# Lead pair of an attention and affine-MLP kernel: another order of two weight sums, one block cast by its own load, batch 3 loaded and flipped at other places, and its a2 blocks turned by TensorE

## The chip, the core and the metric

The kernel runs on one NeuronCore of a Trainium2 chip. A core has five engines with instruction streams of their own: TensorE (PE, with its weight loads as PEld), VectorE (DVE), ScalarE (ACT), GpSimd (POOL) and SyncE (SP, which here only issues transfers). Transfers run on 16 DMA engines; those issued by SP go to the hardware queue q1, those issued by POOL to the software queue q0, which also cast float32 to bfloat16 on the way and can add to what is in DRAM. The metric is the time of one launch in microseconds, the median of several runs.

## What is computed

Grouped attention for 8 batches (16 query heads, 4 key and value heads, 384 tokens, head size 64), and behind it one layer of a residual MLP with affine norms:

```python
scores = scale * np.matmul(q, k.transpose(0, 1, 3, 2))
attn = softmax(scores);  x = attn @ v                    # (8, 384, 1024)
a1 = alpha1 * x + beta1
tok = np.einsum('ts,bsd->btd', w_tok, a1)
u = x + lam * tok
a2 = alpha2 * u + beta2
ch = np.maximum(a2 @ w_ch1, 0.0) @ w_ch2                 # 1024 -> 4096 -> 1024
out = u + lam * ch
```

(`softmax` stands for the four lines that subtract the maximum, exponentiate, sum and divide.) The two channel products are most of the arithmetic.

## The kernel before

**Pairs.** Batches are taken two at a time. For a pair, each of the two channel products is done with seven half-size products in place of eight, the scheme of Strassen and Winograd: the two batches are the two row blocks of the left matrix, and the weight matrix has four blocks, for W2 named "11", "12", "21", "22" (half of the 4096 rows, half of the 1024 columns). The right-hand sums are S5 = B12 - B11, S6 = B22 - S5, S7 = S6 - B11 and S4 = B21 - S6. `sum_w2(o, c)` (L491) makes quarter c of S_o on DVE with one subtraction (L494), in place: S5 and S6 overwrite B12, S7 overwrites B11, S4 overwrites a second copy of B21, named "again". Then `keep_w2` (L488, issued at L489 on SP) stores the quarter to a DRAM buffer w2s, from which pairs 2 to 4 load all seven right-hand matrices. The plain blocks B11 and B22 are stored too. So the lead pair makes the sums, and the later pairs only fetch them.

**The lead pair.** Attention of batches 0 and 1 runs ahead, up to about 68 us. The first product of the pair (`first_product`, matmuls at L635) follows, then the second product (`second_product`, matmuls at L706, C<-...), which takes the seven products in the order S1 (B11), B21, S5, B22 as o = 3, S6, S7, S4 in 21 turns of 16 matmuls with 512 columns each. Between them the attention of the *next* pair, batches 2 and 3, is woven in: `side(b)` gives the places of the score matmuls (L254), of `av` (L289), of the token mix `tok` (L318, L322), and of what turns its result a2 over so that channels are on partitions. `pair(0)` yields after every four matmuls of the second product, and a hand-written plan, `put(ps, phase, place, function, arguments)`, says what is recorded at each yield. Here ps is the pair, phase 0 its first and phase 1 its second product. Places of batch 2's side are counted from 0, those of batch 3 from 38. The order on every engine is the order in which this plan records the instructions; nothing is reordered later. An engine waits at its own next instruction, so what is behind that instruction waits too.

**Slots.** Weights sit in six ring slots (tile w) and three pad slots, 512 KB each. `pump()` hands a freed slot to the next entry of one queue: the W1 chunks of the first product, the quarters of "21", "12", "22" and "again", then the first four W1 chunks of pair 2 (0, 8, 1, 9). B11 goes to a home of its own in the arena. A slot is freed when the last matmul that reads it is recorded, or in `last_w2` when S4's quarter has been made from it.

**B12's quarters.** `cast_w2("12", c)` (L474, on POOL, in the first product) copies a quarter from the float32 weights into a DRAM buffer raw12 as bfloat16; `load_w2` (L484, on SP) brings it from there to a slot. "21" and "again" work the same way, from w2s. "11" and "22" are cast by their own load, on POOL (L486).

**Batch 3.** Nine loads (`load_next`, L430, POOL) bring keys, queries and values. `flip_q` (L174) and `flip_k` (L170) transpose them by DMA, issued on SP. The token result u is spilled to DRAM (L221, SP), and a2 = u * alpha2 (L328) is turned over in one of two ways: by a DMA transpose on SP (L331), or by three TensorE transposes (`turn`, L392) and an ACT copy out of PSUM (L394). For batch 3 the last three of eight blocks are turned by TensorE, for batch 2 none. `sums_a` (L442 to L444, DVE) makes pair 2's left-hand sums from the turned blocks; it is put at places 76, 79 and 81. `sum_w1` (L505, L510, DVE) makes pair 2's first right-hand sums from W1 chunks.

**Results.** `scaled` multiplies a finished block by lam on POOL (L744) and adds it to the output with an accumulating transfer (L436, POOL).

Of the kernel before, what the change touches and what calls it, by code (L numbers as in the profile page):

```python
# [13 lines left out]
def kernel(  # L14
# [21 lines left out]
    nc = tc.nc  # L36
    f32 = mybir.dt.float32
    bf = mybir.dt.bfloat16
# [11 lines left out]
    P = 128  # L50
    NST = S // P
    NDT = DM // P
    NNT = DFF // P
    NDW = DM // 512
    NP = Hq // 2
    D1 = D + 1
    CW = 2
# [37 lines left out]
    turn, a2_turn = [0], [0]  # L95
# [20 lines left out]
    snaps = hTf.bitcast(f32)  # L116
    SLOTS = 7 * NH // 4
    w2s = [tc.dram_tile([P, NDT * CW * P], bf, name=f"w2s{i}") for i in range(SLOTS)]
    raw12 = [tc.dram_tile([P, NDT * CW * P], bf, name=f"raw12_{i}") for i in range(4)]
    PLACE2 = {o: i for i, o in enumerate((1, 2, 6, 5, 3, 7, 4))}  # L120

    def by_tok(ap):
# [85 lines left out]
    def side(b):  # L208
        vb = vt[b % 2]
        ess, avs, a1s, a2s, xr = {}, {}, {}, {}, {}  # L210
        first, fold = b < 2, b < 4
# [167 lines left out]
        def flip(p):  # L379
            if not first:  # L380
                spill(p)
            if not by_pe(p):
                a2_transpose(p)

        def by_pe(p):
            return b == 0 or b % 2 and p >= NP - (4 if first else 3)

        def turn(p, tag="tp"):
            ps = tp_ps([P, NST, P], tag) if first else three()[:, 0].rearrange("p a b -> p (a b)").bitcast(bf)[:, :S].rearrange(
# [9 lines left out]
        at = {}  # L399

        def put(k, *m):
            at.setdefault(k, []).append(m)
# [3 lines left out]
        for p in range(NP):  # L406
            put((4, 10, 14, 18, 24, 29, 33, 35)[p], av, p)
            put((8, 15, 17, 22, 27, 32, 36, 38 if b % 2 else 39)[p], tok_flip, p)
            if by_pe(p):
                put((36, 39, 41)[p - NP + 3], turn, p)  # L410
        return at

    def loads(b):
# [49 lines left out]
    def home(c):  # L463
        return arena[:, HOME + c * 2048:HOME + (c + 1) * 2048]

    def w2_block(name, c):
        kh, dw = int(name[0]) - 1, int(name[1]) - 1
        return w2src[:, kh * NH + 4 * c:kh * NH + 4 * c + 4, dw * 512:(dw + 1) * 512]

    def stored(name, c):  # L470
        return raw12[c] if name == "12" else w2s[4 * PLACE2[2] + c]

    def cast_w2(name, c):
        nc.gpsimd.dma_start(out=stored(name, c).rearrange("p (a c) -> p a c", a=4), in_=w2_block(name, c))  # L474

    def load_w2(name, c, slots=None):
        if slots is None:
            raw[name, c] = None, home(c)
        else:
            slot = slots.pop(0)  # L480
            raw[name, c] = slot, place(slot)
        at = raw[name, c][1]
        if name in ("21", "again", "12"):
            nc.sync.dma_start(out=at, in_=stored(name, c))  # L484
        else:
            nc.gpsimd.dma_start(out=at.rearrange("p (a c) -> p a c", a=4), in_=w2_block(name, c))  # L486

# [29 lines left out]
    def place(slot):  # L517
        return ring[:, slot] if slot < RING else pad[:, (slot - RING) * 2048:(slot - RING + 1) * 2048]
# [20 lines left out]
    order0 = EARLY + (0, 1, 2, 3, 4)  # L539
    chunks0 = [*EARLY, *(g + NCH // 2 for g in EARLY), *(c for g in order0[3:] for c in (g, g + NCH // 2))]  # L540
    queue = [(load_w1, c) for c in chunks0[RING:]] + [(load_w2, "21", c, w1_free) for c in range(4)]
    for name, cs, slots in (("12", (0, 1), w1_free), ("12", (2, 3), pad_free), ("22", (0,), pad_free), ("22", (1, 2, 3), w1_free),
                            ("again", (0,), w1_free), ("again", (1,), pad_free), ("again", (2, 3), w1_free)):
        queue += [(load_w2, name, c, slots) for c in cs]
# [356 lines left out]
    with tc.manual_schedule(engines=order):  # L901
# [122 lines left out]
        def put(ps, phase, at, *m):  # L1024
            plan.setdefault((ps, phase, at), []).append(m)

        def put_all(ps, phase, table, at=lambda u: u):
            for u, ms in table.items():
                for m in ms:
                    put(ps, phase, at(u), *m)  # L1030

        def put_flips(ps, phase, b, places):
            for u, m in zip(places, ((flip_k, b), *((flip_q, b, i, 2) for i in range(0, NP, 2)))):
                put(ps, phase, u, *m)
# [13 lines left out]
        put(1, 0, 35, to_all, 1, 1, 1)  # L1048
        put(1, 0, 38, scale_beta)
        for c in range(4):  # L1050
            put(0, 0, 1 + 3 * c, cast_w2, "12", c)
            put(0, 0, 62 + 9 * c, load_w2, "11", c)
            put(0, 1, 29 + 4 * c, keep_w2, 1, c)
            put(0, 1, 38 + 2 * c, keep_w2, 3, c)
            put(0, 1, (11, 12, 16, 18)[c], sum_w2, 5, c)
            put(0, 1, (20, 21, 25, 26)[c], sums_first_hid, 2, c)
            put(0, 1, (28, 30, 31, 34)[c], sums_first_hid, 4, c)
            put(0, 1, (37, 40, 41, 43)[c], sum_w2, 6, c)
            put(0, 1, (44, 45, 49, 50)[c], sums_first_hid, 3, c)
            put(0, 1, (51, 54, 58, 61)[c], sum_w2, 7, c)  # L1060
            put(0, 1, (57, 59, 63, 66)[c], last_w2, c)
        for u, o in ((77, 5), (79, 7), (81, 6)):
            put(0, 1, u, sum_w1, 0, o)
        for ps in range(NB - 1):
            c = 2 * ps + 2
            for i in range(9):
                put(ps, 0, 4 + 6 * i if ps == 0 else 4 + 7 * i, load_next, c, 1)
                put(ps, 1 - (ps > 0), 6 + 2 * i if ps == 0 else 91 + 2 * i, load_next, c + 1, 1)
            put_flips(ps, 0, c, range(76, 86, 2))
            put_all(ps, 1, side(c))  # L1070
            for u, f, h in zip((24, 25, 27, 29, 33, 34) if ps == 0 else (10, 17, 18, 28, 33, 33),
                               (flip_q, flip_k, flip_q, flip_q, flip_k, flip_q), (0, 0, 2, 4, 2, 6)):
                put(ps, 1, u, f, c + 1, h, 2)
            put_all(ps, 1, side(c + 1), lambda u: u + 38)
            for j, u in ((0, 76), (2, 79), (3, 81)):
                put(ps, 1, u, sums_a, j, 1 if j else 2)

        def steps(ps):
            done = [0, 0]
            for second in pair(ps):  # L1080
                for f, *a in plan.pop((ps, second, done[second]), []):
                    f(*a)
                done[second] += 1
                yield
            for key in [k for k in plan if k[0] == ps]:
                for f, *a in plan.pop(key):
                    f(*a)

        first = steps(0)

        def product(n=1):
            for _ in range(n):
                next(first)

        A, C = side(0), side(1)
        lower, upper = range(NP // 2), range(NP // 2, NP)
        A.k_transpose(0, 1)
# [20 lines left out]
        for i, c in zip((28, 30, 32, 34), range(4)):  # L1118
            at.setdefault(i, []).append((cast_w2, "21", c))
# [44 lines left out]
```

## Time and profile before

| | us |
|---|---|
| median of three runs | 763.64 |
| the runs | 757.52, 763.64, 763.93 |
| the profiled execution | 757.84 |
| its span, first to last instruction | 756.1 |
| attention of batches 0 and 1 | up to about 68 |
| lead pair, first product | 68 to 133.6 |
| lead pair, second product with attention of batches 2 and 3 | 133.6 to 251 |
| pair 2 (first and second product) | 251 to 434 |
| pair 3, pair 4 | 434 to 607, 607 to 756 |

A line of the profile names the line of the kernel, the engine, the operation and its tiles, written `out<-in`. "Idle before" is the time that an engine stood before the instruction, and the releaser is what ended it. `SPq`, `POOLq` and so on are the engine's own queue: waits and transfers being issued. The granted clock is the share of full speed that TensorE had. DMA share is the mean busy share of the 16 DMA engines; it can be over 1 because packets of two queues overlap. Tile names are shortened: `a` is a1, `k` is k2, `raw` is raw12, `w` is the ring of weight slots, `pad` the three pad slots, `obuf` holds a2 blocks, `ops` the turned left-hand operands, and `in_moe_w_ch_dram` is either of the weight matrices in DRAM.

### The profile page before, as it was taken

How to read it: one execution, taken by the hardware profiler on the slowest of the kernel's cores; microseconds unless marked ns; L12 is line 12 of the kernel's file. 1: busy time of each engine (PE TensorE's matmuls, PEld its weight loads, DVE VectorE, ACT ScalarE, POOL GpSimd, SP SyncE). 2: the span in 40 equal slices, each digit the busy share in tenths (PEclk: the TensorE clock that was granted, in tenths of full speed). 3: DMA queues.
4: the chain of work that ended last, by engine and by line, in shares of the span. 5: the costliest groups of instructions: out<-in, count | busy, mean ns of one | idle time of the engine just before them, and what ended most of it. 6: DMA issues, size and time to landing. Idle time of an engine off the chain costs nothing.

```text
span 756.1 us, 14435 instructions
## 1 busy us (share of the span) xinstructions
PE 720.0 (95%) x5644; PEld 410.1 (54%) x5703; DVE 547.3 (72%) x1016; ACT 369.6 (49%) x555; POOL 201.0 (27%) x242
## 2 busy tenths in 40 slices
PE   8997999997979799999999999999999999999998
PEld 4664555454535355655555566655555556654444
DVE  8888876485787498756968988765967888762454
ACT  7875766544525266663433266674433356660000
POOL 8753340251025254120002244120102213100011
PEclk9999999999999899999999999999999999999999
DMA  9999999999999999996999999996999999937965
GB/s 165 186 228 241 196 175 233 220 219 172 284 294 262 219 178 186 201 247 166 261 265 161 215 155 176 207 237 207 229 261 183 206 155 132 140 127 282 283 185 104
DMA packets 208465, 155.85 MB, mean 206 GB/s; under 512 B 92685, under 2 KB 186229, under 8 KB 208141
## 3 DMA queue, kind: packets, MB, share of 16 engines
q0 software_dynamic: 118064, 64.47, 65.4%
q1 hardware_dynamic: 89644, 90.01, 44.0%
q8 instruction: 44, 0.72, 0.4%
q10 hardware_dynamic: 688, 0.46, 0.2%
q14 instruction: 25, 0.20, 0.1%
HBM read 157.32 MB, written 41.94 MB: 264 GB/s over the span
## 4 chain that ended last, share of the span: by engine, by line
PE 71%; issue 9%; DVE 7%; DMA 7%; POOL 5%; ACT 1%; POOLq 0%; DVEq 0%; ACTq 0%
PE C L851 27%; PE X L785 15%; PE Y L785 8%; DMA w<-in_moe_w_ch_dram 5%; PE Z L785 4%; PE sc L254 3%; PE C L706 3%; PE sc L289 2%; PE sc L318 2%; PE X L635 2%; PE Y L635 2%; DMA pad<-w2s 1%; DMA ops<-obuf 1%; DVE pad L510 1%; POOL w L183 1%
## 5 line engine op out<-in xcount | busy, mean ns | idle before, releaser
L851 PE MATMUL C<-w,arena 128*128 128x512 bf16 (+2 forms) x711 | 163.7, 372 | 1.6 <-issue 0.3
L263 ACT ACTIVATE es<-sc 128x1024 bf16<-128x1024 f32 x108 | 104.1, 1024 | 121.5 <-PE sc L254 112.9
L851 PEld LDWEIGHTS <-arena 128*128 128x128 bf16 x1040 | 94.7, 98 | 100.6 <-issue 5.1
L436 POOL DMA_DIRECT2D out_dram<-hT x45 | 40.0, 888 | 296.7 <-DVE hT L744 138.1
L790 ACT ACTIVATE hT<-X,bias 128x384 f32<-128x384 f32 x144 | 83.6, 581 | 65.5 <-PE X L785 54.9
L785 PEld LDWEIGHTS <-w 128*128 128x128 bf16 x768 | 75.3, 98 | 56.5 <-DVE w L505 3.2
L183 POOL DMA_DIRECT2D w<-in_moe_w_ch_dram x64 | 60.0, 987 | 152.7 <-DVE xr L325 46.9
L785 PEld LDWEIGHTS <-pad 128*128 128x128 bf16 x576 | 56.8, 99 | 39.6 <-issue 3.0
L785 PE MATMUL X<-ops,pad 128*128 128x384 bf16 x384 | 71.5, 330 | 0.0
L785 PE MATMUL X<-ops,w 128*128 128x384 bf16 x384 | 70.2, 326 | 1.0 <-DVE ops L804 1.0
L851 PE MATMUL C<-pad,arena 128*128 128x512 bf16 (+2 forms) x288 | 69.5, 373 | 0.4
L706 PEld LDWEIGHTS <-arena 128*128 128x128 bf16 x336 | 30.6, 99 | 40.6 <-issue 12.9
L325 DVE TENSOR_TENSOR xr<-sc,xr 128x384 f32<-128x384 f32 x48 | 26.5, 553 | 32.4 <-PE sc L322 18.1
L318 PEld LDWEIGHTS <-wtokT 128*128 128x128 bf16 x576 | 39.0, 98 | 15.4 <-issue 3.2
L785 PE MATMUL Y<-ops,w 128*128 128x384 bf16 x192 | 40.5, 333 | 5.2 <-DVE w L505 2.8
L510 DVE TENSOR_TENSOR pad<-w,pad 128x1024 bf16<-128x1024 bf16 x64 | 44.3, 692 | 0.1
L706 PE MATMUL C<-w,arena 128*128 128x512 bf16 x161 | 41.0, 383 | 2.3 <-DMA w<-in_moe_w_ch_dram 1.8
L254 PE MATMUL sc<-qT,kT 64*128 64x384 bf16 (+2 forms) x504 | 38.0, 275 | 4.9 <-DMA kT<-k 2.4
L792 DVE TENSOR_TENSOR arena<-Y,hT 128x384 bf16<-128x384 f32 x48 | 26.5, 556 | 17.8 <-ACT hT L790 15.8
L785 PE MATMUL Z<-ops,w 128*128 128x384 bf16 x192 | 39.0, 326 | 0.0
L289 PEld LDWEIGHTS <-es 128*128 128x128 bf16 x864 | 32.8, 97 | 11.3
L263 ACT ACTIVATE hT<-sc 128x1024 bf16<-128x1024 f32 x36 | 35.7, 1036 | 4.4 <-PE sc L254 4.3
(181 smaller groups left out, 1143.1 us busy)
## 6 DMA issues: line engine op xcount, KB each, us to landing
w<-in_moe_w_ch_dram POOLq DMA_DIRECT2D x67, 512.0 KB, 10.6
w<-w2s SPq DMA_DIRECT2D x67, 512.0 KB, 4.9
pad<-w2s SPq DMA_DIRECT2D x25, 512.0 KB, 4.8
out_dram<-hT POOLq DMA_DIRECT2D x45, 256.0 KB, 7.0
out_dram<-xr SPq DMA_DIRECT2D x48, 192.0 KB, 6.1
q_raw<-in_q_dram POOLq DMA_DIRECT2D x28, 192.0 KB, 8.5
w2s<-w SPq DMA_DIRECT2D x10, 512.0 KB, 4.6
w2s<-arena SPq DMA_DIRECT2D x8, 512.0 KB, 9.5
```

Of the source, the lines that this page charges most:

```text
L183: nc.gpsimd.dma_start(out=w1[:, w1_slots[c]], in_=w1src[:, :, c * CW * P:(c + 1) * CW * P])
L254: nc.tensor.matmul(out=sc[:, hh, k % 4:k % 4 + n], lhsT=kT_[r, 2 * p // G, BLK[hh][sk], :], rhs=qT_[r, p, st:st + n, :], start=True, stop= ...
L263: nc.scalar.activation(out=e, in_=sc, func=EXP, scale=scale_qk)
L289: nc.tensor.matmul(out=av[:, hh, sq, :], lhsT=ess[k // 4][:, m % 2, k % 4, :], rhs=vb[:, sk, hk, :], start=(sk == 0), stop=(sk == NST - 1))
L318: nc.tensor.matmul(out=ps[:, tt, :], lhsT=wtokT[:, st, tt * P:(tt + 1) * P], rhs=a1s[p][:, st, :], start=(st == 0), stop=(st == NST - 1 an ...
L436: nc.gpsimd.dma_start(out=by_tok(out[b])[:, ms, dw * 512:(dw + 1) * 512], in_=o, accum_op=ADD)
L510: tt(out=t, in0=x, in1=y, op=SUB)
L635: nc.tensor.matmul(out=ps[:, :n], lhsT=tb[G, o][:, dt, e * P:(e + 1) * P], rhs=opb(FIRST1[o], n)[:, dt], start=(o in (1, 2, 7) and dt == 0 ...
L706: nc.tensor.matmul(out=x, lhsT=lead_hid[:, t, FIRST2[o], ms * P:(ms + 1) * P], rhs=rhs[:, t % 4 * 512:(t % 4 + 1) * 512], start=(o in (1, ...
L785: nc.tensor.matmul(out=ps, lhsT=tb[g, o][:, dt, e * P:(e + 1) * P], rhs=opb(LEFT1[o])[:, dt], start=(o in (1, 2, 7) and dt == 0), stop=(dt ...
L790: nc.scalar.activation(out=snap[o, e], in_=ps, func=IDENT, bias=hi if o == 5 else lo)
L851: nc.tensor.matmul(out=x, lhsT=hid[:, t, LEFT2[o], ms * P:(ms + 1) * P], rhs=rhs[:, t % 4 * 512 + c0:t % 4 * 512 + c1], start=((not last o ...
```

## The change

All edits touch the lead pair.

```diff
-    raw12 = [tc.dram_tile([P, NDT * CW * P], bf, name=f"raw12_{i}") for i in range(4)]
...
         def by_pe(p):
-            return b == 0 or b % 2 and p >= NP - (4 if first else 3)
+            return b in (0, 3) or b % 2 and p >= NP - (4 if first else 3)
...
             if by_pe(p):
-                put((36, 39, 41)[p - NP + 3], turn, p)
+                put((11, 18, 20, 25, 30, 36, 39, 41)[p], turn, p)
...
-        if name in ("21", "again", "12"):
-            nc.sync.dma_start(out=at, in_=stored(name, c))
+        if name in ("21", "again"):
+            nc.sync.dma_start(out=at, in_=stored(c))
         else:
             nc.gpsimd.dma_start(out=at.rearrange("p (a c) -> p a c", a=4), in_=w2_block(name, c))
...
         for c in range(4):
-            put(0, 0, 1 + 3 * c, cast_w2, "12", c)
             put(0, 0, 62 + 9 * c, load_w2, "11", c)
-            put(0, 1, 29 + 4 * c, keep_w2, 1, c)
+            put(0, 1, (41, 43, 45, 47)[c], keep_w2, 1, c)
...
-            put(0, 1, (51, 54, 58, 61)[c], sum_w2, 7, c)
-            put(0, 1, (57, 59, 63, 66)[c], last_w2, c)
+            put(0, 1, (51, 54, 57, 58)[c], sum_w2, 7, c)
+            put(0, 1, (60, 62, 64, 66)[c], last_w2, c)
...
-                put(ps, 1 - (ps > 0), 6 + 2 * i if ps == 0 else 91 + 2 * i, load_next, c + 1, 1)
+                put(ps, 1 - (ps > 0), i if ps == 0 else 91 + 2 * i, load_next, c + 1, 1)
...
-            for u, f, h in zip((24, 25, 27, 29, 33, 34) if ps == 0 else (10, 17, 18, 28, 33, 33),
+            for u, f, h in zip((14, 16, 18, 27, 32, 33) if ps == 0 else (10, 17, 18, 28, 33, 33),
                                (flip_q, flip_k, flip_q, flip_q, flip_k, flip_q), (0, 0, 2, 4, 2, 6)):
```

1. S7's third and fourth quarter are made at places 57 and 58 (58 and 61 before), and S4's quarters, with the slots that they free, at 60, 62, 64 and 66 (57, 59, 63 and 66 before). On DVE all four quarters of S7 now stand ahead of the first of S4. B11's four quarters are stored at places 41 to 47, not 29 to 41.
2. B12's quarters are loaded by POOL with a cast straight from the float32 weights. The buffer raw12, four POOL casts and four SP loads are gone. In POOL's order the four loads stand between B11's quarters and the first of B22.
3. Batch 3's nine loads are put at places 0 to 8 instead of every second place from 6 to 22, and its flips at 14, 16, 18, 27, 32 and 33 instead of 24, 25, 27, 29, 33 and 34.
4. All eight a2 blocks of batch 3 are turned by TensorE and copied by ACT. Five DMA transposes leave SP's queue, 15 TensorE transposes and five ACT copies come in.

On SP the lead pair has nine transfers fewer, on POOL as many as before. The order in pairs 2 to 4 is the same.

More of the change, by code (lines that the diff above doesn't have):

```diff
@@ L468, in w2_block, with stored @@
         return w2src[:, kh * NH + 4 * c:kh * NH + 4 * c + 4, dw * 512:(dw + 1) * 512]
-    def stored(name, c):
-        return raw12[c] if name == "12" else w2s[4 * PLACE2[2] + c]
+    def stored(c):
+        return w2s[4 * PLACE2[2] + c]
     def cast_w2(name, c):
-        nc.gpsimd.dma_start(out=stored(name, c).rearrange("p (a c) -> p a c", a=4), in_=w2_block(name, c))
+        nc.gpsimd.dma_start(out=stored(c).rearrange("p (a c) -> p a c", a=4), in_=w2_block(name, c))
     def load_w2(name, c, slots=None):
```

## The prediction

> **What bounds the kernel now.** First the page: one engine sets the end.
>
> ```profile
> PE 720.0 (95%) x5644; PEld 410.1 (54%) x5703; DVE 547.3 (72%) x1016; ACT 369.6 (49%) x555; POOL 201.0 (27%) x242
> ```
>
> TensorE (PE) is busy 720 of 756 us. From 265 us on, the chain of waits is an unbroken run of PE matmuls, and the change leaves pairs 2 to 4 as they are, so only the stretch up to 265 us matters. Second, busy time by stage from the end of the lead pair's first product on (columns: stretch, length, PE, PEld, DVE, ACT, POOL busy with instructions, granted clock, DMA share, GB/s):
>
> ```profile
> 133.60:180.00 46.40, 45.25 (x430) 25.14 (x436) 31.32 (x51) 24.01 (x31) 17.71 (x19) 1.00 1.14 207
> 180.00:192.00 12.00, 7.64 (x55) 4.07 (x55) 4.12 (x7) 4.26 (x6) 0.00 (x0) 0.86 1.24 204
> 192.00:218.00 26.00, 25.79 (x239) 14.32 (x241) 21.62 (x33) 13.93 (x19) 0.00 (x0) 1.00 0.95 318
> 218.00:230.00 12.00, 6.62 (x56) 3.35 (x56) 8.68 (x9) 2.71 (x5) 8.42 (x8) 0.86 1.15 230
> 230.00:251.00 21.00, 20.17 (x180) 11.31 (x181) 12.97 (x20) 9.48 (x15) 8.32 (x8) 1.00 1.27 246
> 251.00:266.00 15.00, 10.11 (x46) 4.75 (x44) 8.51 (x18) 4.23 (x8) 3.53 (x5) 0.77 1.25 223
> ```
>
> Three holes: A (180-192) with 4.4 us idle, B (218-230) with 5.4, C (251-266) with 4.9. After each the clock stands at half for 3.4, 3.4 and 6.8 us (share 0.86, 0.86, 0.77). PE is busy in about 2.6, 3.2 and 5.0 us of that, and half of it is lost: 1.3, 1.6, 2.5. So A costs 5.7, B 7.0, C 7.4: 20.1 us. Third, the waits of PE name the causes:
>
> ```profile
> PE C L706 <- DVE arena L494: 5.2, 1, 5.2
> PE Y L785 <- DVE w L505: 2.8, 1, 2.8
> PE sc L254 <- DMA kT<-k: 2.4, 1, 2.4
> PE C L706 <- DMA w<-in_moe_w_ch_dram: 1.8, 2, 1.3
> PE Y L785 <- DVE ops L443: 1.1, 1, 1.1
> PE X L785 <- DVE ops L804: 1.0, 1, 1.0
> ```
>
> A is the flip of batch 3's keys (2.4) and quarters of B22 (1.8). B is S7's last quarter, C the sums for pair 2. Fourth, the timeline of DVE says what DVE itself stood at:
>
> ```profile
> 218.93 1.23 DVE L494 TENSOR_TENSOR pad<-pad,w 128x2048 bf16<-128x2048 bf16 x1 [1.89 <-DMA pad<-w2s]
> 221.13 2.92 DVE L494 TENSOR_TENSOR arena<-pad,arena 128x2048 bf16<-128x2048 bf16 x1
> ...
> 252.58 0.56 DVE L442 TENSOR_TENSOR ops<-ops 128x768 bf16<-128x768 bf16 x1 [6.33 <-DMA ops<-obuf]
> ...
> 263.37 0.69 DVE L510 TENSOR_TENSOR pad<-w 128x1024 bf16<-128x1024 bf16 x1 [4.77 <-DMA w<-in_moe_w_ch_dram]
> ```
>
> The first line is S4's second quarter, queued ahead of S7's last (the second line), waiting for a copy of B21. At 252.58 it is a transpose of batch 3 by DMA (issued on SP at 236.7), at 263.37 a W1 chunk.
>
> **Part by part.** I count the second product in steps of four matmuls (LDWEIGHTS of L706 by fours): step 37 is at 180.9, 58 at 212.1, 63 at 218.8, 80 at 247.8. Where I say when a transfer moved, I took a queue's packets in order and gave each transfer its bytes.
>
> *S7 ahead of S4.* S7's third and fourth quarter no longer stand behind S4's second, so B's cause goes. What is late next is in the same edit: B11's four stores move from plan places 29-41 to 41-47, and S7 overwrites B11. On SP the last of them now stands behind 14 half-megabyte transfers that become ready from step 37 on (the stores of B22 and of S6, the other B11 stores, three B21 loads). The trace has 15 such transfers with flips and spills between them moving from 190.9 to 219.7 us, nearly alone on the DMA engines: about 1.5 us each. Fifteen of them, two or three spills and two transposes make 26 us, so the last B11 store lands 28 to 31 us after step 37. Step 58, where S7's last quarter is queued on DVE, is 25 us after step 37 without hole A, and PE needs the quarter at step 63, 32 us after. It takes 1.2 us, or 2.9 when a POOL multiply runs beside it (the row at 221.13, with L744 at 221.68 on POOL). Behind it on DVE are S4's first quarter and block 3's sums, which the new TensorE turn at that step waits for. A remainder of 0 to 7; I take 3, nearest to the row of 1.5 us. Gain 4.0.
>
> *B12 by its own load.* Four casts into DRAM go (L474, in the first product, where PE waits for no load), and four SP loads at 132-134. Instead POOL issues four casting loads (0.75 us each) once the slots come free, from 131 us. The nearest row is B11's, same size and source: back to back with the queue empty they moved in 2.7 us each (111.8, 114.3, 117.0). With B22's first quarter that is 134 to 148 us; DVE needs the quarters at 149.2, 150.3, 155.9, 158.1. I price it at nothing, hidden under the last steps of S1 and the first of B21; if the queue ran as slowly as at 220-250 (6.5 us a load), the last would land at 160 and hold DVE, and with it TensorE, some 2 to 5 us. The page lists 10.6 us to landing for POOL's weight loads and 4.9 for SP's. The Trainium skill, DMA: Bandwidth & Descriptors, section Issuing engine by pattern, puts simple loads on Sync and calls that path generally faster; by it alone each quarter would come 5.7 us later, which still is before three of the four uses.
>
> *Batch 3 sooner.* Its nine loads go out at about 136-143 instead of 135-160, no longer behind POOL's wait at L744 (11.4 us); nine loads at 0.5 to 1.2 us follow B22's first quarter, so keys are in at about 151, queries by 158, against 145.7 and 165. The first three flips are queued nine or ten places earlier, the others one or two. Now the first key flip is issued at 169.5 and moved until 186; then it should be done near 165. The B22 quarters, issued at 165-168 as before because their slots set that, find a shorter queue: they moved until 183-188 and PE asks at 181.6-183.2. At 3.5 us each after two stores the last lands at 180-184. A leaves 0 to 3; I take 1. Gain 4.7. SP's wait for the query load at the first flip (up to 7 us, place 14) holds batch 2's spills, and xr has four buffers, some 15 us of steps: hidden unless that wait passes 15.
>
> *All a2 blocks by TensorE.* Adds 15 transposes on PE: three take 0.17 us between neighbours at 245.8, so 0.9 us for five turns, all on the path, and 5 x 0.48 us on ACT (L394, hidden: ACT is half idle there). It takes five DMA transposes off SP (0.5 us of data each alone, up to 2.8 under load, 2 to 14 us to land), so L442 runs at about step 76. What is late next in C is W1 chunk 9: its slot frees at step 80, it was issued at 249.2, began to move at 257.9 behind two chunks and four stores, and was used at 263.4. These waited in turn for POOL's load at 220.8, held by the store of B22's last quarter; that store now lands about 22 us after step 37, not 38, so the queue should be short at step 80 and the chunk in 8 to 10 us after it instead of 15; PE wants L804 10 us after step 80. A remainder of 0 to 7; I take 2.4. Gain 5.0.
>
> The sum: 4.0 + 4.7 + 5.0 - 0.9 = 12.8 us off the profiled 757.84 (span 756.1): 745.0. The median, 763.64, is 5.8 above that execution (the runs were 757.52, 763.64, 763.93), so 750.8 for the median; I say 750.
>
> The half clock is part of the sum because the profile's clock row shows it behind all three holes, behind C from 255.0 us although no wait there is over 2.84 us. The Trainium skill, TensorE: Matmul & The Clock Gate, section What's actually happening, has the clock drop after an idle window of about 3.4 us. By it A and C, whose waits are all shorter, would have no half clock to give back, 3.8 us less, and the sum would be 9.0; the trace disagrees.
>
> **The rivals.**
> 1. *B11's stores become the wait.* For: SP issued its stores up to 14 us after their plan places at 190-210. Against: three flips and two B11 stores fewer stand in that stretch. B's whole 4.0 is not won, and DVE's lag takes 1 to 2 more: 756 (median). Chance 0.17.
> 2. *Chunk 9 stays late.* For: it cannot be issued before step 80, and at 10.6 us (the page's median) plus 1.4 us to the issue and 1.6 on DVE it is 4 late. Against: the queue ahead of it shortens. C gives 0 to 1: 755. Chance 0.13.
> 3. *DMA is full and the waits only change names.* The edits add four loads at 2.7 us and take four at 1.8 and five transposes, so little work leaves; the DMA share is over 1.1 in most stages. Against: 0.95 at 192-218, and stores and loads are spread more evenly. Nothing won: 760 to 764. Chance 0.07.
> 4. *Slower: SP stuck at the first query flip.* If B12's loads push batch 3's query load past 166 us (they add 11 us to queue 0), SP stands for over 15 us from place 14; spills land late, av waits for xr, and the stores behind slide past S7. Price: A and C stay as they are, B grows from 7 to about 10.5, the turns add 0.9: 4.4 over the median, 768. For: one queue holds both. Against: that queue moved 0.1 MB in 130-140. Chance 0.08.
>
> **How the numbers follow.** The forecast has 0.55: 745 to 754 for the median, 739 if the runs fall with the faster group. Its lower end takes all remainders near 0, its upper end about 1.5 times those taken. Range 740 to 758: it leaves out rivals 3 and 4 and a little at each end; with A, B and C all at their upper bounds the time is 761, which lies with rival 3. One per cent is 7.6 us, about what can be told from no change here. Faster by that: the forecast (0.53), half of rival 1 (0.08) and most of 2 (0.09): 0.70. Slower: rival 4: 0.08. Same: 0.22.
>
> **What would show it.** Right: in the stage around step 63 DVE no longer waits for pad<-w2s; kT<-k is gone from PE's waits; L442 starts within 2 us of step 76; clock share near 1.00 at 180-192. Wrong: L494 waiting for a store w2s<-arena (rival 1), L804 or L510 still 4 us late (2), L494 waiting at S5 for the loads of B12, or SP at L174 for over 15 us (4). A hole elsewhere of over 3 us would break the sum.

## The result, and the profile after

The changed kernel took 752.7 us (median of 12 runs, 746.38 to 757.16) against 762.11 us for the kernel before, run beside it; ratio 0.9895, 95% interval [0.986, 0.9931]. In a second group of runs it was 0.9907 [0.9871, 0.9942]. So it is about 1% faster, near the forecast of 750, but not in the way that the sum had it. The execution profiled first took 756.5 us (span 754.7), a long one for this kernel; the one profiled in the second group took 751.69, near its median of 751.95. Both are used below, and where they differ, both numbers stand.

The changed kernel does the same work 3 to 9 us later than the kernel before, so the stages must be cut by the work: here from step 36 to 40, from 63 to 66, and 15 us from step 83 on (columns as before):

```profile
182.50:198.60 16.10, 8.65 (x57) 4.12 (x54) 3.63 (x7) 4.83 (x7) 0.00 (x0) 0.72 1.24 204
...
227.80:235.70 7.90, 4.78 (x44) 2.31 (x41) 7.79 (x11) 3.94 (x6) 5.77 (x6) 1.00 1.18 296
...
255.40:270.40 15.00, 13.89 (x84) 8.01 (x83) 10.15 (x18) 8.54 (x15) 8.26 (x11) 1.00 1.33 186
```

C is nearly closed and B has become smaller: 1.1 us idle in C, where 4.9 were, and 3.1 us in B, where 5.4 were (0.6 and 1.5 in the second group), and the clock no longer drops there. A has grown: TensorE is idle for 7.5 us (6.2 in the second group), where 4.4 were, and the clock share is 0.72. The waits of TensorE in the changed kernel (engine, line, tile, releaser: us in total, times, longest):

```profile
PE sc L253 <- DVE xr L296: 4.4, 3, 3.4
PE C L705 <- DMA w<-in_moe_w_ch_dram: 3.6, 2, 2.3
PE sc L391 <- DVE obuf L327: 2.3, 1, 2.3
PE X L784 <- DVE ops L803: 1.1, 1, 1.1
...
PE C L705 <- DVE arena L493: 0.6, 1, 0.6
```

The key flip's 2.4 us in A are gone, as said. In their place stand the B22 quarters, twice as long as before (3.6 against 1.8), and a wait that the trace of before hardly had: scores (L253) for a division of `av` (L296, DVE), 3.4 us of it in A. In the second group that wait is 5.1 us in A, and the B22 quarters cost 0.6. The timeline of DVE in the changed kernel says what that division stood at, and what else DVE waited for in B and C:

```profile
193.48 0.56 DVE L296 TENSOR_TENSOR xr<-sc,rinv 128x384 f32<-128x384 f32 x1 [10.60 <-DMA out_dram<-xr]
...
227.23 1.23 DVE L493 TENSOR_TENSOR arena<-pad,arena 128x2048 bf16<-128x2048 bf16 x1 [1.72 <-DMA w2s<-arena]
...
261.95 0.69 DVE L509 TENSOR_TENSOR pad<-w 128x1024 bf16<-128x1024 bf16 x1 [4.61 <-DMA w<-in_moe_w_ch_dram]
```

The first row: `xr` has four buffers, and DVE stood 10.60 us until a spill of u had left one of them. The second is the store of B11 in front of S7's last quarter, small as forecast. The third is W1 chunk 9, which now comes just in time: TensorE loses 1.1 us behind it (the L803 row of the waits), and lost 1.0 there before.

To compare kernels I cut the span at the steps (four matmuls of the second product each). A is the time from step 36 to 40, B from 63 to 66, C from 83 to pair 2's second product. Outside these columns the kernels take the same times within 2 us, but for the start of step 0, which lies between 132.8 and 137.6 us in these executions.

| kernel | median, us | ratio to before [95%] | profiled | A | 40 to 63 | B | C |
|---|---|---|---|---|---|---|---|
| before | 758.14 to 762.11 | 1 | 757.84 | 11.41 | 27.99 | 11.05 | 83.07 |
| changed | 752.7 | 0.9895 [0.986, 0.9931] | 756.50 | 16.10 | 29.20 | 7.90 | 76.49 |
| changed, second group | 751.95 | 0.9907 [0.9871, 0.9942] | 751.69 | 14.16 | 30.01 | 6.15 | 75.86 |
| 1 undone | 757.21 | 0.9987 [0.996, 1.0014] | 756.10 | 17.80 | 28.49 | 11.19 | 75.11 |
| 2 undone | 745.93 | 0.9854 [0.9803, 0.9905] | 744.47 | 5.63 | 28.49 | 10.68 | 75.20 |
| 3 undone | 753.1 | 0.9932 [0.9902, 0.9961] | 749.47 | 8.13 | 30.76 | 11.19 | 75.10 |
| 4 undone | 762.86 | 1.0048 [1.0016, 1.008] | 765.86 | 13.99 | 30.69 | 7.68 | 84.79 |
| 2 alone | 758.99 | 0.9985 [0.9954, 1.0016] | 761.89 | 13.00 | 28.49 | 8.02 | 85.44 |
| 1 and 4 alone | 753.57 | 0.9933 [0.9902, 0.9964] | 755.16 | 13.42 | 29.86 | 11.25 | 75.21 |
| B22 by scratch instead of B12 | 748.2 | 0.9848 [0.9812, 0.9883] | 747.16 | 5.63 | 31.85 | 8.84 | 75.22 |
| 2 and B11's stores undone | 743.58 | 0.979 [0.9753, 0.9826] | 742.56 | 5.63 | 28.49 | 8.89 | 75.21 |
| the same, S7 sooner | 743.3 | 0.9815 [0.9772, 0.9858] | 741.60 | 5.63 | 28.49 | 5.22 | 78.05 |
| the same, turn at place 66 | 744.72 | 0.9822 [0.9789, 0.9856] | 742.99 | 6.43 | 28.49 | 5.12 | 77.93 |

The shortest that any kernel shows is 5.6 for A, 5.1 for B and 75.1 for C. The changed kernel still has 8.5 to 10.5 us to give in A.

### The profile page after: what moved, and what is told of

It is laid out like the page before. It is cut to its first block, busy times and chain, and to the rows that moved or that the text cites. A ratio compares the mean times of both kernels' runs of the same rounds, so it can differ in the third digit from the quotient of the medians.

```text
span 754.7 us, 14520 instructions
## 1 busy us (share of the span) xinstructions
PE 723.2 (96%) x5718; PEld 410.4 (54%) x5718; DVE 546.8 (72%) x1016; ACT 372.5 (49%) x560; POOL 201.8 (27%) x242
## 4 chain that ended last, share of the span: by engine, by line
PE 76%; DVE 8%; DMA 6%; POOL 4%; issue 3%; ACT 1%; SPq 1%; DVEq 0%; POOLq 0%; ACTq 0%
PE C L850 29%; PE X L784 15%; PE Y L784 8%; PE Z L784 4%; PE C L705 4%; PE X L634 4%; PE sc L253 3%; PE sc L288 3%; PE Y L634 3%; PE sc L317 2%; DMA out_dram<-xr 2%; DMA ops<-obuf 1%; DVE pad L509 1%; DMA w2s<-arena 1%; DMA w<-in_moe_w_ch_dram 1%
## 5 line engine op out<-in xcount | busy, mean ns | idle before, releaser
L850 PE MATMUL C<-w,arena 128*128 128x512 bf16 (+2 forms) x744 | 168.4, 372 | 0.0
L784 PEld LDWEIGHTS <-w 128*128 128x128 bf16 x768 | 75.1, 98 | 52.8 <-issue 1.6
L253 PE MATMUL sc<-qT,kT 64*128 64x384 bf16 (+2 forms) x504 | 38.5, 274 | 5.8 <-DVE xr L296 4.4
```

Source lines behind the costliest of these rows:

```text
L253: nc.tensor.matmul(out=sc[:, hh, k % 4:k % 4 + n], lhsT=kT_[r, 2 * p // G, BLK[hh][sk], :], rhs=qT_[r, p, st:st + n, :], start=True, stop= ...
L784: nc.tensor.matmul(out=ps, lhsT=tb[g, o][:, dt, e * P:(e + 1) * P], rhs=opb(LEFT1[o])[:, dt], start=(o in (1, 2, 7) and dt == 0), stop=(dt ...
L850: nc.tensor.matmul(out=x, lhsT=hid[:, t, LEFT2[o], ms * P:(ms + 1) * P], rhs=rhs[:, t % 4 * 512 + c0:t % 4 * 512 + c1], start=((not last o ...
```

## The experiments

**Each edit undone, one at a time.** The edits are numbered as in the section on the change. First S7's and S4's places, with B11's stores:

```diff
-            put(0, 1, (41, 43, 45, 47)[c], keep_w2, 1, c)
+            put(0, 1, 29 + 4 * c, keep_w2, 1, c)
...
-            put(0, 1, (51, 54, 57, 58)[c], sum_w2, 7, c)
-            put(0, 1, (60, 62, 64, 66)[c], last_w2, c)
+            put(0, 1, (51, 54, 58, 61)[c], sum_w2, 7, c)
+            put(0, 1, (57, 59, 63, 66)[c], last_w2, c)
```

> The changed kernel with the first edit undone: S7's and S4's quarters and B11's stores at their old places. The changed kernel stands at 0.9895 of the kernel before. Theory T (the gain is C plus B, and A got worse through batch 3's flips standing ahead of the spills on SP): hole B comes back, PE waits some 5 us at L705 for DVE L493, and the time is 3 to 5 us over the changed kernel, a ratio of 0.993 to 0.996. Rival R (B was only traded for other waits, the new stores of B11): ratio stays at 0.988 to 0.991.

Measured 0.9987 [0.996, 1.0014], more than the expected 0.993 to 0.996; B is back at 11.19, with the wait that it had before (waits of TensorE in this kernel):

```profile
PE C L705 <- DVE arena L493: 5.1, 1, 5.1
```

Beside the other three, the edit is worth 3.3 to 5.0 us of B, and about 0.8 to 0.9% by the ratios (0.9895 and 0.9907 with it); part of that is A, which is 1.7 to 3.6 us longer here (17.80) for a reason that was not looked for. Then B12 through the scratch buffer again:

```diff
-        if name in ("21", "again"):
-            nc.sync.dma_start(out=at, in_=stored(c))
+        if name in ("21", "again", "12"):
+            nc.sync.dma_start(out=at, in_=stored(name, c))
...
+            put(0, 0, 1 + 3 * c, cast_w2, "12", c)
```

> The changed kernel with B12 again cast into DRAM by POOL and loaded by SP. Theory T: A's new wait is made by the flips and not by B12's loads, so A stays within 2 us of the changed kernel's (step 36 to 40 in 16 us) and the ratio at 0.987 to 0.993. Rival R2 (the four casting loads in queue 0 delay B22's quarters and batch 3): A shrinks by 4 us or more, the ratio falls to 0.983 to 0.986.

Measured 0.9854 [0.9803, 0.9905]: the rival's time, and A decides it, which fell from 16.10 (14.16 in the second group) to 5.63, with no wait of TensorE left in it. The theory that the flips make A's wait, and not the loads of B12, fell here. Then batch 3's places:

```diff
-                put(ps, 1 - (ps > 0), i if ps == 0 else 91 + 2 * i, load_next, c + 1, 1)
+                put(ps, 1 - (ps > 0), 6 + 2 * i if ps == 0 else 91 + 2 * i, load_next, c + 1, 1)
...
-            for u, f, h in zip((14, 16, 18, 27, 32, 33) if ps == 0 else (10, 17, 18, 28, 33, 33),
+            for u, f, h in zip((24, 25, 27, 29, 33, 34) if ps == 0 else (10, 17, 18, 28, 33, 33),
```

> The changed kernel with batch 3's loads and flips at their old places. Theory T: the spills are no longer behind flips, DVE does not wait for out_dram<-xr before L296, step 36 to 40 takes 11 us or less instead of 16, and the time is 3 to 5 us under the changed kernel, a ratio of 0.983 to 0.986. Rival R3 (A is as long in either placing, and the 16 us of the profiled execution was that execution's): the ratio stays at 0.988 to 0.992. If the third edit is what won A, as predicted: 0.994 to 0.997.

Measured 0.9932 [0.9902, 0.9961], so between the second and the third expectation: A fell to 8.13, but B rose to 11.19 and the stretch before it to 30.76. With the second edit in place, the third wins nothing in A: it is longer with it. In time this hardly shows (0.9932 without the third edit, 0.9895 and 0.9907 with it), because with the short A the last two quarters of S7 wait 3.0 and 2.3 us for B11's stores, and B is long again. And the turns:

```diff
-            return b in (0, 3) or b % 2 and p >= NP - (4 if first else 3)
+            return b == 0 or b % 2 and p >= NP - (4 if first else 3)
```

> The changed kernel with only the last three a2 blocks of batch 3 turned by TensorE, the first five by DMA transposes again. Theory T: hole C comes back (L441 waits for a transpose that lands some 13 us after its issue), 6.5 us, against 0.9 us of turns saved: ratio 0.995 to 0.998. Rival R4 (C went because queue 0 was emptier, not because of the turns): C stays short, ratio 0.987 to 0.990.

Measured 1.0048 [1.0016, 1.008], more than was expected. C is back, longer than before, and its timeline row on DVE names the cause in a line:

```profile
261.05 0.56 DVE L441 TENSOR_TENSOR ops<-ops 128x768 bf16<-128x768 bf16 x1 [8.73 <-DMA ops<-obuf]
```

The sums for pair 2 wait for a DMA transpose of batch 3, as they did for 6.33 us before. The fourth edit is worth 8.3 to 8.9 us in C.

**Is it the load of B12 itself?** The kernel before with the second edit alone, with the changed kernel in the same group:

```diff
-    raw12 = [tc.dram_tile([P, NDT * CW * P], bf, name=f"raw12_{i}") for i in range(4)]
...
-        if name in ("21", "again", "12"):
+        if name in ("21", "again"):
...
-            put(0, 0, 1 + 3 * c, cast_w2, "12", c)
```

> The changed kernel itself, beside the three other kernels of this group. Both theories: 0.986 to 0.993 of the kernel before, hole A (places 36 to 40) 14 to 17 us long, B (63 to 66) 7 to 9, C (place 83 to the second pair) 76 to 77.

> The kernel before with the second edit alone: B12's quarters by their own casting loads on POOL's queue, everything else as before. Theory (that load is what lengthens A, whatever else is done, because batch 3's loads stand behind it on POOL): A grows from 11.4 to 14 or more, B and C stay at 10 to 12 and 82 to 84, time 1.003 to 1.010 of the kernel before. Rival (it costs only together with batch 3's loads brought forward into the same places): A stays at 10.5 to 12.5, time 0.997 to 1.002.

The changed kernel came in at 0.9907, with A as expected and B and C up to 1 us under what was expected. The second edit alone: 0.9985 [0.9954, 1.0016], and A at 13.00, 1.6 over the kernel before. The time is the rival's, A lies between the two (B and C moved as well, by -3.0 and +2.4, which was not expected). Alone the load costs nothing that the times can tell. The other half of the question is the third edit without the second, that is, edits 1 and 4 alone (the second and third diffs above together):

> Second and third edits undone: B12 by the scratch copy, batch 3's loads and flips at their old places; the first and fourth edits stand. Theory (the third edit does win hole A, once B12's loads are out of POOL's queue): A is 9.5 to 12 long, against 5.6 with the third edit; time 0.985 to 0.992 of the kernel before. Rival (A is short because batch 3's transposes are gone from SP's queue by the fourth edit, and the third wins nothing): A is 5.6 to 7.5, time 0.979 to 0.983.

Measured 0.9933 [0.9902, 0.9964], A 13.42, both just above the theory's bounds, and TensorE waits 4.5 us there for two B22 quarters. That completes a square, with the first and fourth edit in all four:

| | B12 by the scratch copy | B12 by its own load |
|---|---|---|
| batch 3 at its old places | A 13.42, ratio 0.9933 | A 8.13, ratio 0.9932 |
| batch 3 sooner | A 5.63, ratio 0.9854 | A 14.16 and 16.10, ratio 0.9907 and 0.9895 |

The third edit wins 7.8 us in A without the second and loses 6 to 8 with it. The second is worth nothing in time beside the old places, and costs 0.4 to 0.5% beside the new ones (there the intervals of the ratios overlap; the lengths of A do not).

**What collides.** Rows of POOL's timeline, first with B12 by the scratch copy (second edit undone), then in the changed kernel of the second group:

```profile
137.53 2.97 POOL L430 DMA_DIRECT2D q_raw<-in_q_dram  x4 [0.61 <-issue]
...
145.04 0.75 POOL L430 DMA_DIRECT2D v<-in_v_dram  x1 [3.81 <-DMA pad<-in_moe_w_ch_dram]
146.65 0.74 POOL L430 DMA_DIRECT2D v<-in_v_dram  x1 [0.86 <-DMA k<-in_k_dram]
149.84 2.11 POOL L744 TENSOR_TENSOR hT<-hT,vecs 128x512 f32<-128x512 f32 x1 [2.44 <-ACT hT L718]
```

```profile
139.91 0.75 POOL L429 DMA_DIRECT2D q_raw<-in_q_dram  x1 [0.99 <-DMA w<-in_moe_w_ch_dram]
142.43 0.74 POOL L429 DMA_DIRECT2D q_raw<-in_q_dram  x1 [1.78 <-DMA w<-in_moe_w_ch_dram]
144.93 0.74 POOL L429 DMA_DIRECT2D q_raw<-in_q_dram  x1 [1.76 <-DMA pad<-in_moe_w_ch_dram]
147.85 0.74 POOL L429 DMA_DIRECT2D v<-in_v_dram  x1 [2.18 <-DMA pad<-in_moe_w_ch_dram]
150.39 0.74 POOL L429 DMA_DIRECT2D v<-in_v_dram  x1 [1.80 <-DMA pad<-in_moe_w_ch_dram]
151.42 0.74 POOL L429 DMA_DIRECT2D v<-in_v_dram  x1 [0.29 <-DMA k<-in_k_dram]
152.18 1.28 POOL L743 TENSOR_TENSOR hT<-hT,vecs 128x512 f32<-128x512 f32 x1
```

In the changed kernel each load of batch 3 from the second query load on waits on POOL until an earlier one has landed, five times a quarter of B12 or B22. It is always the transfer eight places before it: the ninth waits for the first, the tenth for the second. In the trace POOL's transfers use eight completion semaphores in turn, and a load waits for the transfer that had its semaphore before. With each queue's packets taken in order, these transfers moved as follows (us):

```
                                  2 undone         changed, second group
B12's four quarters               (on SP's queue)  135.9 to 146.4
last value load of batch 3        150.8 to 153.7   161.7 to 163.1
second result of S1, added        159.4 to 161.0   164.8 to 171.0
first key flip of batch 3         162.9 to 164.1   167.4 to 171.2
second query flip                 166.8 to 167.9   180.8 to 186.2
the spill that the division needs 169.4 to 172.5   186.0 to 188.8
B22's second to fourth quarter    168.0 to 182.0   170.9 to 184.5
```

With the second edit undone POOL's queue is empty from 161 to 168 us, both flips move before B22's quarters start, and the spill lands at 172.5. In the changed kernel both queues come to 171 with work left, and then B22's quarters and the flips move at the same time. The Trainium skill, DMA: Bandwidth & Descriptors, section Issuing engines are not separate DMA queues, says that transfers issued by SP and by GpSimd run on the same 16 DMA engines and interleave; the trace agrees, with a query flip that takes 1.1 us before B22's loads and 5.4 beside them. The spill, queued behind that flip, lands 13.5 us after its issue, and the division waits for its buffer:

```profile
189.08 0.56 DVE L296 TENSOR_TENSOR xr<-sc,rinv 128x384 f32<-128x384 f32 x1 [8.67 <-DMA out_dram<-xr]
```

If that is so, any four quarters taken off POOL's queue should do. In the next kernel it is B22 that goes by the scratch copy, and B12 keeps its own load:

```diff
-        if name in ("21", "again"):
-            nc.sync.dma_start(out=at, in_=stored(c))
+        if name in ("21", "again", "22"):
+            nc.sync.dma_start(out=at, in_=stored(name, c))
...
+            put(0, 0, 1 + 3 * c, cast_w2, "22", c)
```

> The changed kernel with B22 instead of B12 by a scratch copy (cast in pass 1, loaded by SP); B12 keeps its own casting load. Theory 1 (A is long because B22's quarters come last in POOL's queue of transfers, behind B12's and batch 3's): A falls from 16 to 5.5 to 8.5, time 0.979 to 0.985. Theory 2 (A is long because B12's quarters hold POOL, so that batch 3's loads, and behind them the flips and the spills on SP's queue, come late): A stays at 11 to 16, time 0.987 to 0.993.

Measured 0.9848 [0.9812, 0.9883], A 5.63. POOL was held just as long there (the first result went out at 154.6 us, against 154.2), and A closed all the same; so theory 2, that POOL's own delay makes the hole, fell. The first key flip is no sooner there (it had moved by 172), but the query flip behind it moved in 2.1 us, with POOL's queue empty, and the spill had moved by 177.6, where it took until 188.8. So what makes the hole is late flips that move at the same time as B22's cast loads. Whether it is the casting, or only that four more loads are on the DMA engines at that time, no run separates. Some of the gain was lost behind it: places 40 to 63 took 31.85, and DVE stood 3.42 us at a store of B11.

**What is left in B.** With the second edit undone B was 10.68. Rows of DVE in that kernel:

```profile
211.06 1.34 DVE L494 TENSOR_TENSOR arena<-pad,arena 128x2048 bf16<-128x2048 bf16 x1 [2.04 <-DMA w2s<-arena]
214.39 1.23 DVE L494 TENSOR_TENSOR arena<-pad,arena 128x2048 bf16<-128x2048 bf16 x1 [1.99 <-DMA w2s<-arena]
```

S7's last two quarters wait 2 us each for B11's stores, which edit 1 had put later: rival 1 of the prediction. In the changed kernel they cost DVE 1.72 us (nothing in the second group), and the long A, which lets TensorE come to B that much later, is the likely cover. It is not shown, and a long A is not enough: with edits 1 and 4 alone A is 13.42, and DVE waits 2.4 and 2.7 us for those stores. With the stores at their old places as well:

```diff
-            put(0, 1, (41, 43, 45, 47)[c], keep_w2, 1, c)
+            put(0, 1, 29 + 4 * c, keep_w2, 1, c)
```

> The changed kernel with B12 by the scratch copy again (second edit undone) and B11's four stores at their old places (29, 33, 37, 41). Theory (B's remainder of 10.7 us with the second edit undone is S7's two quarters waiting 2.0 us each for those stores, plus the half clock behind it): A stays at or under 6.5, B falls to 5 to 7.5, C stays at 75 to 76, time 0.976 to 0.982. Rival (B is the wait for the turned a2 blocks, 2.3 us, and the half clock behind that): B stays above 9.5, time 0.984 to 0.989.

Measured 0.979 [0.9753, 0.9826], the best ratio of all, clear of the changed kernel in the same group. But B fell only to 8.89, between the two expectations. The store waits are gone; a 2.6 us wait for a turned a2 block stays, and DVE's rows show what that block stood behind:

```profile
208.86 4.28 DVE L494 TENSOR_TENSOR arena<-pad,arena 128x2048 bf16<-128x2048 bf16 x2
213.07 0.68 DVE L721 TENSOR_TENSOR hT<-C,hT 128x512 f32<-128x512 f32 x1
213.67 1.99 DVE L494 TENSOR_TENSOR w<-w 128x2048 bf16<-128x2048 bf16 x1
215.58 0.54 DVE L325 TENSOR_TENSOR xr<-sc,xr 128x384 f32<-128x384 f32 x1
216.16 1.32 DVE L328 TENSOR_TENSOR obuf<-xr,vecs 128x384 bf16<-128x384 f32 x1
```

Two S7 quarters and S4's first, which take 1.22 us each elsewhere, took 4.28 and 1.99 here, 2.6 us too long. Two kernels try it from two sides, both with the last two edits kept undone. One puts S7's quarters sooner, the other the turn later:

```diff
-            put(0, 1, (51, 54, 57, 58)[c], sum_w2, 7, c)
+            put(0, 1, (47, 50, 53, 56)[c], sum_w2, 7, c)
```

> The second edit and B11's stores undone, as in the fastest kernel so far, and S7's quarters at places 47, 50, 53 and 56 instead of 51, 54, 57 and 58, so that VectorE does them before POOL's additions begin at place 60. Theory (what is left of B is VectorE's backlog: the S7 quarters took 4.28 us for two, 1.99 and 1.21 beside POOL's additions, where one elsewhere takes 1.22): the quarters take 1.22 to 1.3 each, the 2.6 us wait for the turned a2 block is gone, B falls from 8.9 to 4 to 6, time 0.972 to 0.977. Rival (VectorE has no room before place 60 either: the quarters then hold up the attention's divisions and the wait only moves to places 48 to 60): places 40 to 63 grow from 28.5 to over 31, time 0.978 to 0.984.

```diff
-                put((11, 18, 20, 25, 30, 36, 39, 41)[p], turn, p)
+                put((11, 18, 20, 28, 30, 36, 39, 41)[p], turn, p)
```

> The second edit and B11's stores undone, as in the fastest kernel so far, and the fourth turn of batch 3 three places later (66 instead of 63). Theory of the backlog: TensorE passes place 63 and waits for the division of the next block instead (its scores waited for that until 219.4 us, 1.9 us after the turn); B stays at 8 to 9, time 0.978 to 0.981. Rival (the turn stands too near to the block that it turns, and that alone makes the wait): the 2.6 us wait and the half clock behind it go, B falls to 4 to 6.5, time 0.972 to 0.976.

Measured 0.9815 [0.9772, 0.9858] and 0.9822 [0.9789, 0.9856]. In both, B closed, to 5.22 and 5.12. With S7 sooner the quarters took 1.22 us each and the wait for the turn was 0.3, as the backlog theory said, though the time came out above its 0.972 to 0.977 (the 1.99 that its expectation counts with S7 is S4's first quarter, which took 2.70 there). With the turn later B came out as the rival said, and the time above its 0.972 to 0.976; but in that execution the two S7 quarters took 2.36 together, so it does not tell whether the turn's place would do with slow ones, and the two causes of the last 3.7 us of B stay unseparated. Neither kernel is faster than the one that they start from, since C grew by 2.8 and 2.7 us and the steps from 66 to 83 by 1.0 and 1.2. In the kernel with S7 sooner DVE's timeline has, at the start of pair 2,

```profile
246.73 0.69 DVE L510 TENSOR_TENSOR pad<-w 128x1024 bf16<-128x1024 bf16 x1 [6.16 <-DMA w<-in_moe_w_ch_dram]
```

where the kernel without it has 3.11 us for the same row, at 247.54. TensorE came to pair 2 four us sooner, and W1 chunk 9 only one. So the transfer of that chunk seems to set the end of this stretch now; that B has nothing more to give until it comes sooner was not tried.

## Why the prediction came out as it did

The time was right, the sum was not, and that the two agree is in good part luck: 12.8 us were to come off the profiled execution, and 1.3 (first group) or 6.2 us (second) did. By its steps:

- *S7 ahead of S4*: gain of 4.0 forecast, 3.2 and 4.9 measured in B. The remainder in the first group was the store of B11, as named, with 1.72 us on DVE, and 2.3 us of TensorE's wait for the turned block behind it; in the second group DVE did not wait for that store, and the turn alone was left (1.2 us). The gain is not this edit's own, though: with the edit as it stands B was 10.68 without the second edit, 11.19 without the third and 11.25 without both.
- *B12 by its own load, priced at nothing*: **this is the step that failed.** Its facts held: the quarters moved in 2.6 to 2.8 us each by 146.4 in the second group, and no sum S5 waited for them; alone, the edit costs nothing. What the step left out is who stands behind the quarters on POOL and on the DMA engines. The pricing asked when B12 is needed, and not when the nine loads of batch 3, put at the same places by the third edit, get through. Beside the third edit this load makes A 8.5 to 10.5 us longer (14.16 and 16.10 against 5.63), where the sum had nothing.
- *Batch 3 sooner*: gain of 4.7 forecast, a loss of 4.7 and 2.75 measured. The working was right for a kernel without the second edit, where the step wins 7.8 us, more than was forecast. It took B22 to "find a shorter queue", last quarter at 180 to 184; it came at 190.8 in the first profiled execution and at 184.5 in the second. And the step did see that the four buffers of `xr` hide a delay of some 15 us only, but looked for it at SP's wait for a query load. The spills were late because the flips in front of them moved slowly.
- *All a2 blocks by TensorE*: gain of 5.0 forecast, 6.6 and 7.2 measured in C, and 8.3 to 8.9 by the experiment. The price of 0.9 was about right: three turns lengthen places 40 to 63 from 27.99 to 28.49 us in the kernels that have no hole in A, 0.17 each. Chunk 9 came much as before, with 4.61 us of DVE's wait (4.77 before) and 1.1 us for TensorE (1.0 before): the gain is that of the transposes that are gone.
- *Half clock*: after the change the clock drops behind A alone (0.72 from step 36 to 40, 0.71 in the second group). B and C, with waits of 2.3 and 1.1 us, show full clock, so those gains include the half clock, as the sum had it. The window of about 3.4 us that the Trainium skill gives (TensorE: Matmul & The Clock Gate, What's actually happening) does not fit all rows: behind the longest waits in A, 3.35 and 5.14 us, the clock dropped, but in the kernel with the second edit and B11's stores undone it dropped as well behind a single wait of 2.62 us (0.60 from 218 to 222 us). By these rows shorter waits can halve the clock too.
- *The rivals*: the mechanism of rival 4 is what happened in A (the load queue too full, spills late, `av` waiting for `xr`), at another place than it was looked for and for 3 to 5 us of waits, not the whole hole of B. Rival 1 was there in small and came out in full once A was closed. Rival 2 did not come. Of the signs named for being right, DVE's wait for `pad<-w2s` and TensorE's for `kT<-k` are gone, but the clock share at 180 to 192 was 0.91, and pair 2's first sum started 3.0 us after step 76, not within 2.

The measured gain is 9.4 us in the first group (762.11 to 752.7) and 7.1 in the second (759.02 to 751.95), where 13.6 were forecast from the median shown. The number came out near because B and C gave up to 3 us more than the sum had, and because the kernel before ran 1.5 to 4.6 us under that median.

## What to carry to other kernels

An edit that costs nothing by itself can cost what another edit of the same change was to win: where two edits put transfers on one queue at the same places, price them together, by the queue's whole list, and undo them in pairs. When a hole closes, the next stall can already stand behind it: here B11's stores came out when A closed, and a weight chunk when B did. A transfer with few buffers behind it, such as a spill, is priced by what stands in front of it on its queue, even where its own data is ready.

## What the runs showed of the hardware

- A DMA transpose moved several times more slowly while transfers of POOL's queue moved beside it. A query flip of 196 KB moved in 0.7 us with POOL's queue empty (191.0 to 191.7 in the second group) and in 5.4 us beside B22's casts; in the kernel with B22 by the scratch copy a key flip of the same size took 4.8 us (167.4 to 172.1) beside a result that was being added. The casts slowed down as well: a 512 KB quarter took 2.6 to 2.8 us from 136 to 149 us in the second group, while SP's queue moved next to nothing, and 4.0 to 5.9 us from 171 to 184.5, beside transposes, stores and spills. How much of that is due to the transposes alone no run separates.
- VectorE's additions, subtractions and multiplications slow down beside GpSimd's. Take those of DVE that took 0.9 us or more between 130 and 260 us, in the kernel with the second edit and B11's stores undone. None of the 23 without a POOL multiplication beside them took over 1.22 us; of the 11 with one, five took from 1.32 to 3.15 us, and three took 1.04 to 1.09 us where the same instruction alone takes 0.56. The other three were not slowed, and each of them had started before POOL's. POOL's then took 1.74 to 2.17 us, against 1.26 to 1.55 us for the other seven. The Trainium skill, SBUF — State Buffer, section SBUF: two separate sides, has VectorE (with two inputs in SBUF, for one) and GpSimd share a port pair, which the one that starts first holds for its whole instruction while the other is blocked; the trace agrees for ten of the eleven (the one of 3.15 us had started 0.76 us before POOL's and was slowed all the same).
